# Attention and two mixture-of-experts layers on one core: the last unit's input weighted ahead of its split, its last chunk added and stored in one step, q's scale inside its exponential, and another list of steps

## The chip, the cores and the metric

The kernel runs on one core of one Trainium2 chip. The metric is the device time of one execution in microseconds. The kernel before took 541.41, 538.64 and 541.26 us in three runs; the median is 541.26 us.

## What is computed

Three layers follow each other. The first is a linear attention over 4 batches, 8 heads, 576 tokens and a head size of 64, with 128 random features. The second and third are mixtures of 8 experts over the 2304 tokens, in which each token goes through the one expert that its gate prefers:

```python
q_s, k_s = (q * scale, k * scale)
def phi(x):
    proj = np.einsum('bhsd,md->bhsm', x, omega)
    sq = np.sum(x * x, axis=-1, keepdims=True) / 2.0
    h = proj - sq
    h = h - np.max(h, axis=-1, keepdims=True)
    return np.exp(h) / np.sqrt(m)
kv = np.einsum('bhsm,bhsd->bhmd', k_p, v)
num = np.einsum('bhsm,bhmd->bhsd', q_p, kv)
den = np.einsum('bhsm,bhm->bhs', q_p, z)[..., None] + 1e-06
...
for e in range(E):
    h = np.maximum(x[mask] @ w1[e], 0.0)
    ye = h @ w2[e]
    out[mask] = gate_w[mask, None] * eom[mask, e, None] * ye
```

The last line is that of the second layer; the third has the same without `eom`. An expert's matrices are 512 x 1024 and 1024 x 512.

## The kernel before, in words

**Attention.** Two heads of a batch make a `Pair`; there are 16, named 0 to f in the list of steps. A pair is loaded (a, b, c for q, k, v), projected on `om` (the features, scaled by `head_dim ** -0.25`; k in `k_proj`, L184, q in `q_proj`, L218), q's projections are copied out of PSUM (r), their maximum over the partitions is taken on POOL (t), subtracted on DVE (s, L229) and put through an exponential on ACT (x, L233); k goes through a maximum (m, L194) and an exponential (e, L198). Then come the products with v (v), the quotient (n, d, L285 to L289), the turn into the layout of the experts (f, g, `xraw`), and the split of that into a high and a low part (h, l), since the experts' products are made of three fp32r terms: high x high, low x high, high x low.

**Experts.** The most chosen expert of a batch is run on all 576 tokens of that batch as dense work; a table of ones and weights, `cb`, multiplies its result, so that tokens of other experts get zero. Such a run is a `Unit`. There are 8, one per layer and batch, in the order `(0,0) (0,1) (1,0) (1,1) (0,2) (0,3) (1,2) (1,3)`; unit 7, the last, takes its input from unit 5. A unit takes 64 steps of 6 TensorE matmuls of 128x128 by 128x288 each (`run`, L495 to L534): 32 steps up, in 16 groups of 2, and 32 steps down, in 8 groups of 4. Each group fills one of two PSUM banks (`pm`). After an up group ACT takes `hh` out of the bank (L514) and DVE `hl` (L515); after a down group DVE multiplies the bank with `cb` into `y` (L533). A bank is used again two groups later. The weights come in 8 pieces for a unit: fetched (F), cast to the high part `wh` (H, on ACT, or on DVE where the step has a plus, L130 and L132), and their low part `wl` subtracted on DVE (L, L487).

**The tables and the splits.** A gate (flow G) works out a unit's weights on the tokens; its last pieces are small DVE operations (L410 to L424), a transposition on TensorE (`ptc`, L428), a copy to SBUF on ACT (`ct`, L431) and a store to DRAM (`cohd`, L433). Step W (`weigh`, L489) then loads `cb` from `cohd`, spread over all partitions. Both transfers are issued by SP. A first-layer unit's `y` is split for the second layer by X (high, `next_high`) and Y (low, `next_low`, L543).

**The rest.** Tokens that do not go through their batch's chosen expert are gathered into small blocks (flows A and B); in the last unit their results are added to `y` (L758 for the other batches, `merge`, L547 for unit 7's own batch), and `store` (L556) writes the output.

**What sets the order.** `PLAN` is a list of step names that the program walks once; each name emits its instructions on all engines, a number n lets the units' work go on by n steps, `zN` spends N idle matmuls. Each engine runs its own instructions in the order in which they were emitted, and waits in that order; SP does so with the transfers.

Of the kernel before, what the change touches and what calls it, by code (L numbers as in the profile page):

```python
# [23 lines left out]
NF = 128  # L24
# [17 lines left out]
CW = 2 * HD + 4  # L42
TERMS = (0, 0), (0, 1), (1, 0)
# [16 lines left out]
o6 h5 l5 2 f70 g70 f71 q80 q81 r801 ab g71+ G1 G1 o7 r800 r810 h6+ l6 h7+ l7 r811 1 G1 t80 G1 1 t81 S020 G1 G1 2 s80  # L60
# [34 lines left out]
def attention_moe_moe_kernel(ctx, tc, qT, kT, vp, omst, wg1, wg2, w1a, w2a, w1b, w2b, tabs, eye, outT):  # L95
# [41 lines left out]
    class Pair:  # L137
# [667 lines left out]
    with tc.manual_schedule():  # L805
# [54 lines left out]
        for n, u in enumerate(units):  # L860
# [103 lines left out]
```

## Time and profile before

| | |
|---|---|
| runs | 541.41, 538.64, 541.26 us (median 541.26) |
| the profiled execution | 542.26 us, its span on the core 540.4 us |
| TensorE | busy 98% of the span, 5292 matmuls |
| DVE, ACT, POOL | busy 63%, 36%, 13% |

The profile is one execution. Its span is the time from the core's first instruction to its last; the execution's own time has 1.9 us more around it. Busy shares are means over the whole span; the attention ahead of the first unit (the first 54 us) and the units behind it have different limits, so the stretches are to be read apart.

### The profile page before, as it was taken

To read this page: it belongs to the slowest core of one execution; us is meant where nothing else is said; L and a number is where in the kernel's file an instruction comes from. 1 tells how busy PE (TensorE), PEld (TensorE's weight loads), DVE (VectorE), ACT (ScalarE), POOL (GpSimd) and SP (SyncE) were. 2 spreads that over 40 slices of the span, in tenths; PEclk is the share of its full clock that TensorE was granted. 3 is DMA by queue.
4 is the path that set the end of the run, shared out by engine and by line. 5 is a ranking of instruction groups with operands and counts; after the bars stand their busy time and mean duration, and the time that the engine had idled before them with its cause. 6 is when DMAs were issued, how large, how long until landed. Compare 5 with 4: busy or idle time off the path is not lost.

```text
span 540.4 us, 12927 instructions
## 1 busy us (share of the span) xinstructions
PE 529.9 (98%) x5292; PEld 504.7 (93%) x5292; DVE 342.3 (63%) x772; ACT 192.1 (36%) x490; POOL 72.9 (13%) x68
## 2 busy tenths in 40 slices
PE   9999999999999999999999999999999999999995
PEld 6877999899999999999999999999999999999994
DVE  4999663885667867468643456766674368574532
ACT  5887431335325555133320034432330233023100
POOL 5651102230010323020000000500000000021100
PEclk9999999999999999999999999999999999999998
DMA  8547641264426844037234530116425522859421
GB/s 292 186 136 207 194 142 40 90 176 130 102 70 212 253 152 120 30 124 223 92 92 147 128 96 13 55 69 180 124 54 172 174 63 81 269 156 356 162 83 49
DMA packets 83955, 74.18 MB, mean 137 GB/s; under 512 B 14256, under 2 KB 68144, under 8 KB 83888
## 3 DMA queue, kind: packets, MB, share of 16 engines
q1 hardware_dynamic: 83600, 73.15, 43.5%
q8 instruction: 43, 0.70, 0.5%
q14 instruction: 24, 0.20, 0.1%
q10 hardware_dynamic: 288, 0.13, 0.1%
HBM read 57.79 MB, written 15.48 MB: 136 GB/s over the span
## 4 chain that ended last, share of the span: by engine, by line
PE 85%; DVE 8%; DMA 3%; ACT 1%; issue 1%; POOL 1%; POOLq 0%; DVEq 0%
PE pm L91 71%; PE ph L218 3%; PE pn L267 3%; PE ph L184 3%; PE pkv L241 2%; DVE nm L194 2%; DVE qhh L229 1%; DVE wl L487 1%; PE pg L338 1%; DMA wr<-w1a 1%; PE pf L303 1%; DMA wr<-w1b 1%; DMA om<-omst 1%; DVE xt L289 1%; ACT kp L198 0%
## 5 line engine op out<-in xcount | busy, mean ns | idle before, releaser
L91 PE MATMUL pm<-hh,wh 128*128 128x288 f32 x512 | 153.6, 300 | 0.3 <-DVE y L533 0.3
L91 PE MATMUL pm<-xh,wh 128*128 128x288 f32 x512 | 153.0, 299 | 0.3 <-DVE hl L515 0.2
L91 PE MATMUL pm<-xh,wl 128*128 128x288 f32 x512 | 151.0, 295 | 0.0
L91 PE MATMUL pm<-hh,wl 128*128 128x288 f32 x512 | 150.8, 295 | 0.0
L91 PE MATMUL pm<-hl,wh 128*128 128x288 f32 x512 | 150.8, 295 | 0.0
L91 PE MATMUL pm<-xl,wh 128*128 128x288 f32 x512 | 150.8, 294 | 0.0
L515 DVE SCALAR_TENSOR_TENSOR hl<-pm,hh 128x288 fp32r<-128x288 f32 x128 | 58.5, 457 | 83.6 <-ACT hh L514 83.1
L225 POOL PARTITION_ALL_REDUCE qhl<-qhh x32 | 65.0, 2068 | 284.7 <-DVE qhh L130 100.8
L514 ACT ACTIVATE hh<-pm 128x288 fp32r<-128x288 f32 x128 | 52.6, 412 | 137.1 <-PE pm L91 137.0
L91 PEld LDWEIGHTS pm<-xh,wh 128*128 128x128 f32 x512 | 96.1, 188 | 3.9 <-issue 1.6
L91 PEld LDWEIGHTS pm<-hh,wh 128*128 128x128 f32 x512 | 96.1, 188 | 3.3 <-issue 1.8
L91 PEld LDWEIGHTS pm<-hl,wh 128*128 128x128 f32 x512 | 96.1, 188 | 0.0
L91 PEld LDWEIGHTS pm<-xl,wh 128*128 128x128 f32 x512 | 96.1, 188 | 0.0
L91 PEld LDWEIGHTS pm<-xh,wl 128*128 128x128 f32 x512 | 96.1, 188 | 0.0
L91 PEld LDWEIGHTS pm<-hh,wl 128*128 128x128 f32 x512 | 96.0, 188 | 0.0
L487 DVE TENSOR_TENSOR wl<-wr,wh 128x1024 fp32r<-128x1024 f32 (+1 forms) x72 | 79.8, 1120 | 3.2 <-ACT wh L132 2.7
L533 DVE TENSOR_TENSOR y<-pm,cb 128x288 f32<-128x288 f32 x64 | 29.0, 454 | 69.2 <-PE pm L91 63.8
L132 ACT CAST wh<-wr 128x1024 fp32r<-128x1024 f32 (+1 forms) x39 | 36.9, 960 | 51.4 <-PE pm L91 32.2
L198 ACT ACTIVATE kp<-ph,nm 128x128 f32<-128x128 f32 x140 | 39.3, 385 | 12.9 <-DVE nm L194 12.9
L194 DVE TENSOR_REDUCE nm<-ph 128x3 f32<-128x384 f32 (+1 forms) x64 | 27.7, 483 | 4.1 <-PE ph L184 3.9
L229 DVE TENSOR_TENSOR qhh<-qhh,qhl 128x576 f32<-128x576 f32 x32 | 28.9, 907 | 1.0 <-POOL qhl L225 0.9
L233 ACT ACTIVATE qhh<-qhh 128x576 f32<-128x576 f32 x32 | 22.2, 697 | 15.4 <-DVE qhh L229 15.4
(128 smaller groups left out, 435.8 us busy)
## 6 DMA issues: line engine op xcount, KB each, us to landing
wr<-w2a SPq DMA_DIRECT2D x16, 512.0 KB, 3.8
wr<-w2b SPq DMA_DIRECT2D x16, 512.0 KB, 4.5
wr<-w1a SPq DMA_DIRECT2D x12, 512.0 KB, 4.2
wr<-w1b SPq DMA_DIRECT2D x12, 512.0 KB, 4.7
vt<-vp SPq DMA_DIRECT2D x16, 325.0 KB, 4.3
qr<-qT SPq DMA_DIRECT2D x16, 288.0 KB, 3.6
kr<-kT SPq DMA_DIRECT2D x16, 288.0 KB, 4.6
xd<-xraw SPq DMA_DIRECT2D x16, 288.0 KB, 3.0
```

The costliest lines, as they stand in the source:

```text
L91: nc.tensor.matmul(out, ws(*t), xs(*t), start=first and t == terms[0], stop=last and t == terms[-1])
L132: nc.scalar.copy(out=out, in_=in_)
L184: nc.tensor.matmul(pk[j][:, i * NF : (i + 1) * NF], self.kr[r, c0 : c0 + 128], om[r, :], start=True, stop=True)
L194: nc.vector.tensor_reduce(out=nm[:, j, 0:m], in_=pk, axis=AX.X, op=ALU.max, negate=True)
L198: nc.scalar.activation(self.kp[:, c, j * NF : (j + 1) * NF], self.pk[part][j][:, i * NF : (i + 1) * NF], AF.Exp, bias=self.nm[part][:, j, ...
L225: nc.gpsimd.partition_all_reduce(qm, qe, 128, bass_isa.ReduceOp.max)
L229: nc.vector.tensor_tensor(out=qe, in0=qe, in1=qm, op=ALU.subtract)
L233: nc.scalar.activation(qe, qe, AF.Exp)
L487: nc.vector.tensor_tensor(out=wl[:, p], in0=self.raw[i][:, p], in1=wh[:, p].bitcast(F32), op=ALU.subtract)
L514: nc.scalar.activation(hh[:, s], pm, AF.Relu)
L515: nc.vector.scalar_tensor_tensor(out=hl[:, s], in0=pm, scalar=0.0, in1=hh[:, s].bitcast(F32), op0=ALU.max, op1=ALU.subtract)
L533: nc.vector.tensor_tensor(out=y[:, t], in0=pm, in1=self.cb[:, t], op=ALU.mult)
```

## The change

The multiplication of `om` by the scale goes to a copy, `omk`, which only k's projection uses; q is projected on `om` as it is loaded, and its exponential takes `scale=SCALE`. Unit 5's four chunks of `y` are multiplied by unit 7's `cb` (new steps C50 to C53, in place) ahead of their split, so unit 7 needs no multiplication behind its down groups: of its four chunks the first three are copied out of PSUM by ACT, and the last is added straight from PSUM to the block's result and written to `y` in the one operation of `merge`. `cb` gets a second buffer. All else is the list: nearly every step stands in another place.

```diff
-a0 I a1 b0 b1 c0 c1 c2 J a2 a3 a4 b2 b3 b4 b5 c3 c4 c5 z14 q00 q01 k00 r001 r010+ k01 r000 t00 r011+ m00 t01 q10 r101+
...
+a0 I z14 q00 b0 r001 r000+ q01 b1 k00 k01 r010 t00 r011 a1 m00 e000 q10 r100+ z8 q11 r101+ e001 m01 e010 r110 e011 s00
...
-                        pk[j][:, i * NF : (i + 1) * NF], self.kr[r, c0 : c0 + 128], om[r, :], start=True, stop=True
+                        pk[j][:, i * NF : (i + 1) * NF], self.kr[r, c0 : c0 + 128], omk[r, :], start=True, stop=True
...
-            nc.scalar.activation(qe, qe, AF.Exp)
+            nc.scalar.activation(qe, qe, AF.Exp, scale=SCALE)
...
-            self.cb = pl.mp.tile([128, S], F32, tag="cb", name="cb", bufs=1)
+            self.cb = pl.mp.tile([128, S], F32, tag="cb", name="cb", bufs=2)
...
-                    nc.vector.tensor_tensor(out=y[:, t], in0=pm, in1=self.cb[:, t], op=ALU.mult)
+                    if self is not units[-1]:
+                        nc.vector.tensor_tensor(out=y[:, t], in0=pm, in1=self.cb[:, t], op=ALU.mult)
+                    elif c < NDC - 1:
+                        nc.scalar.copy(out=y[:, t], in_=pm)
+                    else:
+                        self.merge(block, c, t, pm)
                     yield
+
+        def scale(self, c):
+
+            y = self.y[c]
+            nc.vector.tensor_tensor(out=y, in0=y, in1=units[-1].cb, op=ALU.mult)
...
-        def merge(self, block, c, t):
-            y = self.y[c][:, t]
+        def merge(self, block, c, t, y=None):
+            out = self.y[c][:, t]
             nc.vector.scalar_tensor_tensor(
-                out=y, in0=block.y[c][:, t], scalar=state[:, 8], in1=y, op0=ALU.mult, op1=ALU.add
-            )
+                out=out, in0=block.y[c][:, t], scalar=state[:, 8], in1=out if y is None else y, op0=ALU.mult, op1=ALU.add
+            )
...
-            nc.vector.tensor_scalar(out=om, in0=om, scalar1=float(HD) ** -0.25, scalar2=None, op0=ALU.mult)
+            nc.vector.tensor_scalar(out=omk, in0=om, scalar1=SCALE, scalar2=None, op0=ALU.mult)
...
+                    if u.b == units[-1].b:
+                        steps[f"C{n}{c}"] = partial(u.scale, c)
```

By engine the list's instructions come to 502 on ACT in place of 493 and 766 on DVE in place of 773; TensorE has the same matmuls and 23 idle ones in place of 25. The experts' matmuls stand in 51 uninterrupted stretches on TensorE in place of 49.

**First place: DVE around the split of the first unit's first weights** (`wh` and `wl`; the rows on `gt`, `g` and `done` are the end of the first unit's gate, those on `rd` and `xt` the last pair's quotient of batch 0). Before:

```order
L194 TENSOR_REDUCE nm<-ph 128x2 x2
L410 TENSOR_REDUCE gt<-ge 72x8
L411 TENSOR_SCALAR gt<-gt 72x8
...
L424 TENSOR_TENSOR g<-g,gt 72x64
...
L289 TENSOR_TENSOR xt<-pn,rd 128x256
L130 CAST wh<-wr 128x512 x2
L487 TENSOR_TENSOR wl<-wr,wh 128x512 x2
L130 COPY xraw<-pf 128x192
L130 COPY qhh<-ph 128x288 x2
L487 TENSOR_TENSOR wl<-wr,wh 128x1024
L515 SCALAR_TENSOR_TENSOR hl<-pm,hh 128x288 x2
```

and in the change:

```order
L290 TENSOR_TENSOR xt<-pn,rd 128x256
L131 CAST wh<-wr 128x512 x2
L488 TENSOR_TENSOR wl<-wr,wh 128x512 x2
L411 TENSOR_REDUCE gt<-ge 72x8
L412 TENSOR_SCALAR gt<-gt 72x8
...
L425 TENSOR_TENSOR g<-g,gt 72x64
L131 COPY xraw<-pf 128x384
L516 SCALAR_TENSOR_TENSOR hl<-pm,hh 128x288
L488 TENSOR_TENSOR wl<-wr,wh 128x1024
L516 SCALAR_TENSOR_TENSOR hl<-pm,hh 128x288
```

The seven gate operations (two shown, four left out, one shown) now stand behind the split of the first piece, and the low part of the second piece stands behind the first group's `hl`. Two casts of `xh<-xraw` that DVE did ahead of this place are on ACT in the change.

**Second place: ACT in the first unit**, where `ct` is copied. Before:

```order
L431 COPY ct<-ptc 64x72
L132 COPY xraw<-pf 128x384
L132 COPY xraw<-pf 128x192
L132 COPY xraw<-pf 128x384
L132 CAST wh<-wr 128x1024
L132 COPY qhh<-ph 128x288
L514 ACTIVATE hh<-pm 128x288 x2
```

and in the change:

```order
L133 CAST wh<-wr 128x1024
L133 COPY qhh<-ph 128x288
L515 ACTIVATE hh<-pm 128x288 x10
L133 CAST wh<-wr 128x1024
L515 ACTIVATE hh<-pm 128x288 x5
L133 CAST wh<-wr 128x1024
L432 COPY ct<-ptc 64x72
L133 CAST wh<-wr 128x1024
L515 ACTIVATE hh<-pm 128x288
```

The copy of `ct` stood ahead of the unit's first group; now it stands behind the fifteenth of its 16 up groups and a weight cast.

**Third place: DVE in the last down groups of unit 6**, between two multiplications of a bank. In the change:

```order
L131 CAST xh<-y 128x576
L554 TENSOR_TENSOR xl<-y,xh 128x576
L535 TENSOR_TENSOR y<-pm,cb 128x288
L488 TENSOR_TENSOR wl<-wr,wh 128x1024 x2
L643 SCALAR_TENSOR_TENSOR order<-ones 128x576
L648 TENSOR_SCALAR sel<-bx,state 128x576
L651 SCALAR_TENSOR_TENSOR order<-ones,sel 128x576
L535 TENSOR_TENSOR y<-pm,cb 128x288
```

Before, these operations had more multiplications between them:

```order
L533 TENSOR_TENSOR y<-pm,cb 128x288
L633 SCALAR_TENSOR_TENSOR order<-ones 128x576
L487 TENSOR_TENSOR wl<-wr,wh 128x512 x2
L543 TENSOR_TENSOR xl<-y,xh 128x576
L533 TENSOR_TENSOR y<-pm,cb 128x288 x2
L487 TENSOR_TENSOR wl<-wr,wh 128x1024
L533 TENSOR_TENSOR y<-pm,cb 128x288 x2
L638 TENSOR_SCALAR sel<-bx,state 128x576
L641 SCALAR_TENSOR_TENSOR order<-ones,sel 128x576
```

Two weight splits and the three operations of a block's ranking (`order`, `sel`) now stand between one multiplication and the next.

## Rows read from the trace of the kernel before

**Rows 1.** Page, part 1: busy us (share of the span) and count by engine.

```profile
PE 529.9 (98%) x5292; PEld 504.7 (93%) x5292; DVE 342.3 (63%) x772; ACT 192.1 (36%) x490; POOL 72.9 (13%) x68
```

**Rows 2.** Stretches: us, busy PE, PEld, DVE, ACT, POOL; PEclk, DMA share, GB/s.

```profile
20.00:40.00 20.00, 19.35 (x375) 16.07 (x375) 18.79 (x49) 17.68 (x57) 11.45 (x6) 1.00 0.37 123
40.00:54.30 14.30, 13.47 (x264) 11.04 (x260) 13.64 (x46) 10.79 (x39) 2.22 (x2) 1.00 0.67 200
```

**Rows 3.** Chain of waits, start and first unit: start us, us, what.

```profile
4.20 0.24 DVE om L822
...
48.60 5.97 DMA wr<-w1a
54.60 1.06 ACT wh L132
55.68 1.87 DVE wl L487
57.55 0.38 DVE hl L515
57.97 33.65 PE pm L91 x252
91.62 1.20 PE ph L218 x8
```

**Rows 4.** TensorE behind two waits: idle time and its end in brackets.

```profile
57.97 0.40 PE L91 MATMUL pm<-xh,wh 128*128 128x288 f32 x1 [0.22 <-DVE hl L515]
...
514.50 0.40 PE L91 MATMUL pm<-hh,wh 128*128 128x288 f32 x1 [0.34 <-DVE y L533]
```

**Rows 5.** Chain of waits at the end of the span.

```profile
533.88 0.47 DVE y L533
534.35 0.02 issue
534.38 0.52 DVE y L547
```

**Rows 6.** Groups on DVE: busy us, mean ns; idle before, what ended it.

```profile
L487 DVE TENSOR_TENSOR wl<-wr,wh 128x1024 fp32r<-128x1024 f32 x56 | 69.7, 1245 | 3.1 <-ACT wh L132 2.7
L533 DVE TENSOR_TENSOR y<-pm,cb 128x288 f32<-128x288 f32 x64 | 29.0, 454 | 69.2 <-PE pm L91 63.8 <-DMA xd<-y 3.9 <-PE pc L380 1.3
L543 DVE TENSOR_TENSOR xl<-y,xh 128x576 fp32r<-128x576 f32 x16 | 11.7, 750 | 3.1 <-ACT xh L132 3.0
L130 DVE CAST xh<-xraw 128x576 fp32r<-128x576 f32 x8 | 3.6, 452 | 0.6 <-ACT xraw L132 0.5
L641 DVE TENSOR_TENSOR_SCAN order<-ones,sel 128x576 f32<-128x576 f32 x1 | 1.4, 1359 | 0.0
```

**Rows 7.** DVE in order of time, 49 to 51 us: start us, us, operation.

```profile
49.23 0.20 DVE L410 TENSOR_REDUCE gt<-ge 72x8 f32<-72x64 f32 x1
...
50.44 0.22 DVE L424 TENSOR_TENSOR g<-g,gt 72x64 f32<-72x64 f32 x1
```

**Rows 8.** Groups on ACT.

```profile
L514 ACT ACTIVATE hh<-pm 128x288 fp32r<-128x288 f32 x128 | 52.6, 412 | 137.1 <-PE pm L91 137.0
L132 ACT CAST wh<-wr 128x1024 fp32r<-128x1024 f32 x31 | 32.5, 1047 | 40.9 <-PE pm L91 21.7 <-DMA wr<-w1b 14.6 <-DMA wr<-w1a 4.4
L431 ACT COPY ct<-ptc 64x72 f32<-64x72 f32 x8 | 1.7, 210 | 6.5 <-PE ptc L428 6.5
```

**Rows 9.** Stores of the gates' tables, source L433.

```profile
L433 SPq DMA_DIRECT2D cohd<-ct x8: 484/494/596, 51.3 to 447.6; - x8
...
DMA to landing us min/median/max: 1.7/3.9/5.5
```

**Rows 10.** Loads and readers of `cb`.

```profile
L533 DVE TENSOR_TENSOR y<-pm,cb x64: 437/457/458, 83.7 to 533.9; 128x288 f32<-128x288 f32 x64
...
DMA to landing us min/median/max: 3.9/4.5/7.1
```

**Rows 11.** Output stores, source L556.

```profile
DMA to landing us min/median/max: 1.9/2.6/7.2
```

More of the change, by code (lines that the diff above doesn't have):

```diff
@@ L42 @@
 CW = 2 * HD + 4
+SCALE = float(HD) ** -0.25
 TERMS = (0, 0), (0, 1), (1, 0)
@@ new lines @@
+S320 re01 re11 te1 xd1 ke1 xd0 L46 re00 re10 te0 2 S330 me1 ee11 2 ee10 nd0 nd1 dd0 se1 H47 se0 ce qf0 qf1 rf01 rf00
+rf10 kf0 kf1 dd1 tf0 rf11 mf0 xe0 tf1 mf1 ef11 ef10 1 L47 ef01 o9 ob 3 ef00 sf0 1 ve0 ve1 xf0 cf vf0 vf1 xe1 sf1 S110
+we+ ne0 xf1 wf+ ne1 nf0 nf1 fd0 de0 fd1 de1 df0 df1 2 gd0 gd1 hd ld fe0 ff0 ff1 gf0 gf1+ fe1 ge0 ge1+ he+ 1 G5 G5 1 of
+G5 G5 1 G5 G5 1 le hf lf 4 P5 G5 1 G5 2 F50 F51 H50+ L50 F52 4 S430 H51 L51 oc 4 H52 L52 G5 3 S400 2 G5 1 F53 H53+ 2
+S420 4 F54 L53 2 F55 G5 3 od 5 H54+ H55+ 2 X40 L54 L55 1 W5 1 F56 Y40 2 G6 H56+ L56 3 F57 X41+ G6 G6 G6 2 Y41 2 G6
@@ L86 @@
+M710 B S710 B B B B B B M700 M720 S720 S700 1 4
 """
@@ L543, in next_low, with fetch_back @@
             nc.vector.tensor_tensor(out=xl, in0=self.y[c], in1=xh.bitcast(F32), op=ALU.subtract)
-        def merge(self, block, c, t):
-            y = self.y[c][:, t]
+        def merge(self, block, c, t, y=None):
+            out = self.y[c][:, t]
             nc.vector.scalar_tensor_tensor(
-                out=y, in0=block.y[c][:, t], scalar=state[:, 8], in1=y, op0=ALU.mult, op1=ALU.add
+                out=out, in0=block.y[c][:, t], scalar=state[:, 8], in1=out if y is None else y, op0=ALU.mult, op1=ALU.add
             )
+        def fetch_back(self, c, t):
+            src = outT[c * 128 : (c + 1) * 128, self.b * S + t.start : self.b * S + t.stop]
+            nc.sync.dma_start(out=self.y[c][:, t], in_=src)
         def store(self, c, t=slice(0, S)):
@@ L556, in store @@
             nc.sync.dma_start(out=dst, in_=self.y[c][:, t])
-        def fetch_back(self, c, t):
-            src = outT[c * 128 : (c + 1) * 128, self.b * S + t.start : self.b * S + t.stop]
-            nc.sync.dma_start(out=self.y[c][:, t], in_=src)
     def left(l):
@@ L809, in attention_moe_moe_kernel @@
         om = const.tile([128, NF], F32, name="om")
+        omk = const.tile([128, NF], F32, name="omk")
         zeros = const.tile([128, 256], BF16, name="zeros")
@@ L870, in attention_moe_moe_kernel @@
                     steps[f"S{n}{c}{s}"] = partial(u.store, c, t)
-                    if last:
+                    if last and c < NDC - 1:
                         steps[f"M{n}{c}{s}"] = partial(u.merge, block, c, t)
                 if u.l == 0:
+                    if u.b == units[-1].b:
+                        steps[f"C{n}{c}"] = partial(u.scale, c)
                     steps[f"X{n}{c}"], steps[f"Y{n}{c}"] = partial(u.next_high, c), partial(u.next_low, c)
```

68 lines of the change are left out of this document (31 added, 37 removed).

## The prediction, made before the change was timed

> **What bounds the kernel now.** I read the engines' busy shares first. TensorE is busy 98% of the span and DVE 63%, ACT 36% [rows 1]. The reader is to see there that only work taken off TensorE, or time in which it stands still, can move the end by much; the change takes no matmul off it but two idle ones. So the question is where TensorE waits, and I went on to the stretches and the chain of waits.
>
> Ahead of the first unit the picture is another one. From 20 to 54 us DVE is busy 18.79 of 20.00 and 13.64 of 14.30 us, ACT 17.68 of 20.00 [rows 2]. TensorE's busy share is high there too, but its matmuls are small and many of them hang on DVE's and ACT's results. The chain enters the experts by a landing of weights at 54.6 us, a cast on ACT (1.06 us), the subtraction on DVE (1.87 us, more than one piece of work) and `hl`; only then, at 57.97 us, comes TensorE's long stretch: 252 matmuls in 33.65 us, 0.1335 us each [rows 3]. A step of six is then 0.80 us, a down group of four steps 3.20 us. From there on the chain is TensorE's, with small gaps. Two of them stand out: 0.22 us behind `hl` at 57.97 and 0.34 us behind `y` at 514.50 [rows 4]. Behind the last matmul come a multiplication (0.47 us), a handover (0.02) and the addition (0.52), and then the last store [rows 5].
>
> The profiled execution took 542.26 us, 1.0 above the median of 541.26. The sum is made against 542.26 and then shifted by 1.0. A measurement of this kernel tells about 0.5%, or 2.7 us, from no change.
>
> **The change part by part.**
>
> *The attention's end.* Three things leave DVE ahead of the first weights' split. The scaling of `om` leaves the path to the first q projection: 0.24 us [rows 3]. Two casts of `xh` go to ACT: 2 x 0.452 = 0.9 us [rows 6]. The gate's last seven operations go behind the split: from 49.23 to 50.66 us, 1.4 us [rows 7]. That is 2.5 us of DVE. The first two pay in full if DVE is the limit, 1.1 us. The third pays only as far as the first piece of weights has landed, since DVE would else stand before it; no row says how early it lies there, but its fetch follows the gate's choice, which comes 0.9 us earlier for the same two casts. I take -2.0, nearer to the whole, as both stretches have DVE at 94 and 95%. The ends are -2.5 and +1.2: ACT gets two casts that, by the 1.047 us of a cast of 1024 columns [rows 8], are some 0.6 us each, and it is busy 88% of the first stretch.
>
> *The wait at 57.97.* The second piece's subtraction moves behind the first group's `hl`, so this wait of 0.22 us goes, with the slow restart behind it: the matmul took 0.40 us by its row. I take -0.4 (ends -0.5 and 0, where the next `hl` is late instead: it now stands behind the subtraction, with one more bank to cover it).
>
> *The last unit's first multiplication.* The wait of 0.34 us at 514.50 goes, because ACT copies the bank (0.41 us by the `hh` row, the same shape [rows 8]) where DVE stood behind a run of additions: -0.5 with the restart. The eight multiplications themselves lay beside TensorE and cost nothing before; the six copies are covered in the same way, by the other bank's 3.20 us. Were the cover gone, one copy would cost its 0.41 us.
>
> *Unit 0's table, the new wait.* Before, the first store of `ct` began at 51.3 us, and `y` first read `cb` at 83.7 [rows 9, 10]. Now the copy of `ct` stands on ACT behind the fifteenth `hh` and a weight cast, so it starts only when 30 of the unit's steps are done. From there: `hh` 0.41, cast 1.05, copy 0.21 [rows 8], store 3.9 [rows 9], load 4.5 [rows 10], multiplication 0.45 [rows 6], and some 0.3 for six handovers at 0.02 to 0.05 us, 10.8 us in all. TensorE can go on until it needs the first down group's bank back, at the end of step 40: 60 matmuls at 0.1335 are 8.0 us, the last pair's q projection that now stands between them is 1.2 (the row at 91.62 [rows 3]), with the changes of work 9.3 us. The stall is 10.8 - 9.3 = +1.5. Behind the waiting multiplication DVE has copies of q's projections and of `kvr`, and TensorE's next work hangs on them, so nothing fills the gap; on SP the loads of the next weights stand behind the table's load, but those are due more than 20 steps later. With the shortest transfers (1.7 and 3.9 us) the chain is 8.0 us and the stall 0; with the longest (5.5 and 7.1) it is 15.0 and the stall +5.7. I take the medians.
>
> What the Trainium skill says of this differs. Its page "DMA: Bandwidth & Descriptors", section "Anatomy of one DMA — SWDGE (gpsimd) path", fits a transfer's time by 2.0 us plus its bytes over 436 GB/s; as an estimate from that page the 18 KB store would take 2.0 and the 295 KB load 2.7 us, there would be no stall, and the sum would be 1.5 us lower. The rows of this case show 3.9 and 4.5, and I go by these.
>
> *More stretches.* TensorE goes two more times from attention to experts' matmuls and back. By the waits above a change costs some 0.1 us each way in idle and restart: +0.4 (0 to +0.9, two waits of 0.22 with their restarts).
>
> *DVE late in unit 6.* Between one multiplication and the next now stand two subtractions and the ranking's three operations: 2 x 1.245 + 2 x 1.36 and, for `sel`, the 0.45 of a cast of the same tile [rows 6], 5.7 us. TensorE has two groups of 3.20 = 6.4 us from the end of one group until it needs that bank's successor back; DVE needs 0.45 + 5.7 + 0.45 = 6.6. The excess of 0.2 and a restart of 0.2 to 0.3 make +0.5 (0, if DVE starts part of it early, to +1.4, if it also waits for the cast of 1.05 behind which the subtractions come).
>
> *The weighting ahead.* Unit 7's table must now be there before unit 5's `y` is split. In the list its transposition ends at step 407 of 512; copy 0.2, an `hh` before it 0.4, store and load 8.4, the multiplication at 0.75 (the row of `xl`, the same tile), a cast 0.6, the subtraction 0.75 [rows 6], unit 6's own `y` behind them 0.45, handovers 0.3: 11.9 us. TensorE needs that `y` by the end of step 424, 17 steps or 13.6 us later. So nothing, with +2.5 as the upper end (12.6 for the two transfers). The second buffer of `cb` is what lets it be loaded while unit 6's is in use.
>
> *The end.* One multiplication of 0.47 and its handover of 0.02 go from the chain behind the last matmul [rows 5]: -0.5. The ends are 0 and -1.2, if the last store also lands at the 1.9 us of the quickest instead of 2.6 [rows 11]. The additions for the other batches and the three whole-chunk merges, seven operations at 0.75, 5.3 us, stand ahead of the last chunk's merges; the block's last product is in the list 15 steps, 12.0 us, before the end, and the first of these merges is due 3.2 us before it, which leaves 3.5 us for POOL between.
>
> *The sum.* -2.0 - 0.4 - 0.5 + 1.5 + 0.4 + 0.5 - 0.5 = -1.0. From 542.26 that is 541.3, and against the median 540.3. This is no change that can be measured.
>
> **The rivals.**
>
> *Faster: the front gives all, and the table is in time.* The front's whole 2.5 in place of 2.0 and a stall of 0 in place of 1.5 give 540.3 - 0.5 - 1.5 = 538.3, just past the bound of 538.55. For it: in eight transfers of each kind the shortest pair leaves 1.3 us of room, and the part of the sum that is only a restart may be nothing. Against it: the medians are above. The Trainium skill's fit for a transfer, named above, is on its side.
>
> *Slower: the table is late by its slowest.* Store and load stand on SP beside fetches of 512 KB weights. With 5.5 and 7.1 us the stall is 5.7 and the time 540.3 + 4.2 = 544.5, with all behind the multiplication on DVE late as well. For it: both of these durations were seen. Against it: in two columns of eight they are the worst. It decides from where the two transfers take 12.1 us together (a stall of 5.2); from 6.9 us on there is a stall at all.
>
> *ACT takes DVE's place in the front.* It is busy 88% there and gets 1.2 us more; then the front is +1.2 in place of -2.0 and the time 543.5, still within the bound. Against it: the chain enters by way of DVE, and ACT is busy only 10.79 of the 14.30 us ahead of the first weights [rows 2].
>
> **How the numbers follow.** The forecast gets 0.40, the rival that is faster 0.30, the late table 0.20, ACT in the front 0.10. Faster by over 0.5% is then 0.30, slower by over 0.5% 0.20, and no change 0.40 + 0.10 = 0.50. The range goes down to 537.0, which is the faster rival with 0.7 more at the last store and 0.6 less for the lump on DVE and the stretches, and up to the late table's 544.5; what lies beyond, a table late in both units or a front that loses and gains at once, I hold for 2 in 10 or less.
>
> **What would show it.** In the changed kernel's profile the first experts' matmul should start about 52.3 us, some 2 before the 54.3 that end the second stretch of now, with no wait of TensorE for `hl` two groups later. A wait of TensorE for `y` of 1 to 2 us should stand near the 40th step of unit 0, ended by a load of `cb`. Late in unit 6 TensorE should wait for `y` for under 1 us. Behind the last matmul one DVE operation of 0.5 us should stand where two stood. If the attention is as long as before, or no wait for `cb` shows in unit 0, the terms -2.0 or +1.5 are wrong; a wait for `y` at another place, which none of these terms has, would make the whole wrong.

## The result: 0.8% slower, and the profile after

The changed kernel took 544.66 us (median of ten runs, 543.66 to 545.47); the kernel before, run beside it ten times, 539.44 (538.64 to 542.20). The ratio is 1.0083, 95% interval 1.0064 to 1.0102: slower by 4.5 us, where 540.3 and no change were forecast. The time lies 0.2 us above the range.

The ten runs of the kernel before also show that the execution profiled before, 542.26 us, was slower than all of them, 2.8 us above their median. A second profile of it (`before_again`, below) fell on one of 539.47 us. The ledger is made against that one; "experts" is from the first to the end of the last expert matmul, "behind" from there to the end of the span.

| us | before, profiled first | before, second profile | changed | changed less second |
|---|---|---|---|---|
| first experts' matmul | 54.31 | 54.19 | 54.36 | +0.2 |
| experts | 479.55 | 479.06 | 481.25 | +2.2 |
| behind | 6.54 | 4.45 | 6.89 | +2.4 |
| span | 540.4 | 537.7 | 542.5 | +4.8 |

So the loss has two halves, in the experts' stretch and behind the last matmul, and the attention gave nothing. The +0.2 of the first row is scatter: the six profiles that start with the old list have that matmul at 53.99 to 55.46 us, the six that start with the new one at 53.80 to 54.78. Of the +2.4 behind the last matmul 1.1 is the later issue of the last store, 1.8 is that it landed 3.5 us behind its issue where the second profile has 1.7, and -0.5 is the rest. The same landing took 3.8 us in the first profile of before, so it is not shown that the change made it slower. The page of the changed kernel shows none of it (parts 1 and 4):

```profile
PE 531.0 (98%) x5290; PEld 505.4 (93%) x5290; DVE 341.2 (63%) x765; ACT 194.1 (36%) x499; POOL 74.6 (14%) x68
PE 88%; DVE 7%; DMA 2%; ACT 1%; issue 1%; SPq 0%; POOL 0%; DVEq 0%; ACTq 0%; POOLq 0%
```

The shares are those of [rows 1]. What differs is where TensorE stands between two experts' matmuls. TensorE in order of time, changed kernel, the matmul behind each of four new waits (a fifth, at 206.56, reads as a start of 206.97 where 206.69 was due; the trace names no wait there):

```profile
246.40 0.40 PE L92 MATMUL pm<-xh,wh 128*128 128x288 f32 x1 [0.45 <-DVE y L535]
278.21 0.40 PE L92 MATMUL pm<-hh,wh 128*128 128x288 f32 x1 [0.42 <-DVE hl L516]
430.35 0.40 PE L92 MATMUL pm<-xh,wh 128*128 128x288 f32 x1 [0.18 <-DVE hl L516]
481.13 0.40 PE L92 MATMUL pm<-xh,wh 128*128 128x288 f32 x1 [0.47 <-DVE y L535]
```

From one matmul's start to the next's these places take 0.74, 0.72, 0.47 and 0.76 us, and the fifth 0.42, in place of 0.13. The waits of [rows 4] are gone. What stood ahead of them differs from place to place. DVE ahead of the first:

```profile
241.55 1.63 DVE L131 CAST wh<-wr 128x1024 fp32r<-128x1024 f32 x1
243.22 1.23 DVE L488 TENSOR_TENSOR wl<-wr,wh 128x1024 fp32r<-128x1024 f32 x1
244.36 0.75 DVE L230 TENSOR_TENSOR qhh<-qhh,qhl 128x576 f32<-128x576 f32 x1
245.03 0.75 DVE L554 TENSOR_TENSOR xl<-y,xh 128x576 fp32r<-128x576 f32 x1
245.88 0.82 DVE L535 TENSOR_TENSOR y<-pm,cb 128x288 f32<-128x288 f32 x2
```

The bank's multiplication stands behind 4.3 us of other work, and both `y` come at once. Of the 4.3 us 0.95 are in no list of steps: the cast takes 1.63 us where the others of its shape take 0.68 to 0.69, though the last weights fetched ahead of it had landed at 235.86. It lies within a maximum that POOL takes over the partitions:

```profile
241.07 2.85 POOL L226 PARTITION_ALL_REDUCE qhl<-qhh  x1
```

A smaller cast at 239.06 (1.37 us where the others take 0.42) lies within the maximum ahead of it (238.75 to 241.17), and each of the two casts ends 0.74 us before its maximum does. In `after_mended` the larger cast comes at 244.41, behind POOL's work, and takes 0.68. That POOL's work holds the cast is as far as these rows go; no run tests it alone. Without the 0.95 us the multiplication would have been in time, since TensorE waited for 0.45.

At 277.1 a gate's copy on ACT, which waits for DVE, stands ahead of the bank's `hh` (the same at 205.4), and at 429.2 a cast on DVE that waits for its weights stands ahead of `hl`:

```profile
277.10 0.26 ACT L367 COPY ls<-pt 72x128 f32<-72x128 f32 x1 [2.04 <-DVE top L366]
429.24 0.69 DVE L131 CAST wh<-wr 128x1024 fp32r<-128x1024 f32 x1 [1.02 <-DMA wr<-w1b]
```

The DVE rows of the last place stand under "Why the prediction was wrong".

Behind the last matmul, the end of the chain of waits, first of the kernel before (second profile), then of the changed kernel:

```profile
513.90 19.34 PE pm L91 x144
...
533.27 0.47 DVE y L533
...
533.76 0.52 DVE y L547
```

```profile
523.67 11.94 PE pm L92 x90
...
535.63 0.52 DVE y L558
```

One operation stands where [rows 5] had two, as forecast. But the last stores, on SP, kernel before (second profile) and changed kernel (the first number is the first issue, the second reaches to the end of the last):

```profile
532.47 2.17 SPq L556 DMA_DIRECT2D outT<-y  x2
534.30 0.33 SPq L556 DMA_DIRECT2D outT<-y  x1
```

```profile
532.27 0.81 SPq L572 DMA_DIRECT2D outT<-y  x2
...
537.31 0.92 SPq L572 DMA_DIRECT2D outT<-y  x2
```

Before, the last store is issued at 534.30, in the moment its addition ends (533.76 + 0.52). Now the addition ends at 536.15, and the two final stores go out at 537.31 and 537.77: SP comes too late. These two stand in the program behind a branch (the fallback that is not taken), and SP's last store ahead of it was issued at 532.65. The trace has SP's comparison for the branch at 533.13 to 533.18 and its next instruction at 536.49; in the second profile of before they are at 528.64 to 528.70 and 531.65.

### The profile page after: what moved, and what is told of

Its sections match the earlier page's. It is cut to its first block, busy times and chain, and to the rows that moved or that the text cites. A ratio compares the mean times of both kernels' runs of the same rounds, so it can differ in the third digit from the quotient of the medians.

```text
span 542.5 us, 12911 instructions
## 1 busy us (share of the span) xinstructions
PE 531.0 (98%) x5290; PEld 505.4 (93%) x5290; DVE 341.2 (63%) x765; ACT 194.1 (36%) x499; POOL 74.6 (14%) x68
## 4 chain that ended last, share of the span: by engine, by line
PE 88%; DVE 7%; DMA 2%; ACT 1%; issue 1%; SPq 0%; POOL 0%; DVEq 0%; ACTq 0%; POOLq 0%
PE pm L92 70%; PE pn L268 3%; PE ph L185 3%; PE pkv L242 3%; PE ph L219 3%; PE pf L304 2%; DVE wl L488 2%; PE pg L339 1%; DVE nm L195 1%; DMA wr<-w1b 1%; DVE qhh L230 1%; DVE wh L131 1%; DMA kr<-kT 1%; PE idle L852 1%; PE pu L707 0%
## 5 line engine op out<-in xcount | busy, mean ns | idle before, releaser
L226 POOL PARTITION_ALL_REDUCE qhl<-qhh x32 | 67.1, 2138 | 280.2 <-ACT qhh L133 137.0
L488 DVE TENSOR_TENSOR wl<-wr,wh 128x1024 fp32r<-128x1024 f32 (+1 forms) x72 | 81.1, 1142 | 7.5 <-ACT wh L133 7.2
L133 ACT CAST wh<-wr 128x1024 fp32r<-128x1024 f32 (+1 forms) x33 | 32.0, 972 | 58.5 <-DMA wr<-w1b 20.8
L535 DVE TENSOR_TENSOR y<-pm,cb 128x288 f32<-128x288 f32 x56 | 25.3, 454 | 42.1 <-PE pm L92 39.4
L199 ACT ACTIVATE kp<-ph,nm 128x128 f32<-128x128 f32 x140 | 41.2, 396 | 7.6 <-DVE nm L195 7.3
L131 DVE CAST wh<-wr 128x1024 fp32r<-128x1024 f32 (+1 forms) x39 | 25.5, 666 | 7.0 <-DMA wr<-w2b 2.8
```

Of the source, the lines that this page charges most:

```text
L131: nc.vector.tensor_copy(out=out, in_=in_)
L133: nc.scalar.copy(out=out, in_=in_)
L199: nc.scalar.activation(self.kp[:, c, j * NF : (j + 1) * NF], self.pk[part][j][:, i * NF : (i + 1) * NF], AF.Exp, bias=self.nm[part][:, j, ...
L226: nc.gpsimd.partition_all_reduce(qm, qe, 128, bass_isa.ReduceOp.max)
L488: nc.vector.tensor_tensor(out=wl[:, p], in0=self.raw[i][:, p], in1=wh[:, p].bitcast(F32), op=ALU.subtract)
L535: nc.vector.tensor_tensor(out=y[:, t], in0=pm, in1=self.cb[:, t], op=ALU.mult)
```

## The experiments

Ratios are to the kernel before in runs on the same chip, with 95% intervals; a profile's numbers are those of one execution. Of each list of steps some of the tokens that differ are shown.

**before_again.** No edit.

> The kernel before, unchanged, for a second profile. Ten runs of it lie at 538.6 to 542.2 us, median 539.4, and the first profile was taken of one at 542.3, so the sum rested on an execution 2.8 us above the median. Theory 1 (the time between quick and slow executions lies ahead of the experts, where the weights' landing at 54.6 us ended the wait): a quick execution starts its experts some 2 us sooner, at about 52, and the rest is the same. Theory 2 (it lies behind the last matmul, in the last store's landing): first experts' matmul at 54.3 as before, and the time behind the last matmul 5 us in place of 6.8. Ratio to itself 1.000 within 0.003.

Measured: 539.7 us, ratio 1.0002 (0.9987 to 1.0016), profile of 539.47. The experts start at 54.19 in place of 54.31 us; the last store lands 1.7 us after its issue in place of 3.8; the wait at 57.97 of [rows 3, 4] is not there, the second piece of weights having landed at 54.13 in place of 54.58. So most of the 2.7 us between the two spans lies behind the last matmul (theory 2), 0.5 in that wait. The wait that the prediction counted as -0.4 comes in some executions and not in others: of the six profiles that start with the old list, late_store's and code_spread_a's have it too.

**list_only.** The new list with the old arithmetic.

```diff
-            nc.vector.tensor_scalar(out=omk, in0=om, scalar1=SCALE, scalar2=None, op0=ALU.mult)
+            nc.vector.tensor_scalar(out=om, in0=om, scalar1=SCALE, scalar2=None, op0=ALU.mult)
...
-                    if self is not units[-1]:
...
+                    nc.vector.tensor_tensor(out=y[:, t], in0=pm, in1=self.cb[:, t], op=ALU.mult)
-A 1 C50 A X50
+A 1 A X50
...
-S720 S700 1 4
+S720 S700 1 M730 4 M731
```

> The new list of steps with the old arithmetic: om scaled in place, no weighting ahead, the last unit multiplied by cb behind its down groups, its last chunk multiplied and then added. Theory 1 (the list costs the time: DVE's order in the experts' groups and the ending): 544 to 546 us, as slow as the changed kernel or 0.5 slower. Theory 2 (the changed arithmetic costs it, by the weighting on DVE ahead of the split): 540 to 541 us.

Measured: 548.98 us, 1.0170 (1.0148 to 1.0191). Slower still than either theory had it: the list is what costs, and without the new arithmetic it is worse by 4 to 5 us more. In its profile 1.6 of them lie in the experts' stretch and 2.0 behind the last matmul's start (9.2 us in place of 7.2), where the multiplications that are back on DVE hold up the block's additions.

**code_only.** The new arithmetic with the old list.

```diff
-G7 L66 F70
+G7 W7 L66 F70
...
-H67+ X50 Y50 1 X51 1 Y51 X52+ 2 A 1 L67 F71 2 Y52 X53+
+H67+ C50 X50 Y50 1 C51 X51 1 Y51 C52 X52+ 2 A 1 L67 F71 2 Y52 C53 X53+
...
-S630 W7 H73
+S630 H73
```

> The new arithmetic with the old list (only the table's load W7 moved ahead behind its gate, C50 to C53 put straight ahead of X50 to X53, and M730 and M731 gone). Theory 1 (the list costs the time): 538.5 to 540 us, at the kernel before or up to 0.9 quicker, for the wait at 514 us (0.5) and one operation behind the last matmul (0.5) go. Theory 2 (the arithmetic costs it): 543 to 545 us, with TensorE waiting for y of unit 6 where the weighting stands on DVE.

Measured: 543.14 us, 1.0062 (1.0045 to 1.0079). Theory 2's number, but not its reason: three weightings stand in a row ahead of one multiplication of unit 6, two of them with a split that waits for ACT, and TensorE waits 2.46 us (TensorE in order of time):

```profile
460.04 0.40 PE L92 MATMUL pm<-hh,wh 128*128 128x288 f32 x1 [2.46 <-DVE y L535]
```

Behind that wait its clock falls (stretches; the eighth number is the granted clock):

```profile
450.00:457.00 7.00, 7.00 (x55) 7.00 (x54) 5.35 (x20) 1.09 (x3) 0.00 (x0) 1.00 0.45 108
460.00:463.90 3.90, 3.86 (x17) 3.86 (x18) 3.83 (x9) 0.00 (x0) 0.00 (x0) 0.56 0.31 91
```

Of the next 16 intervals between matmuls 15 are 0.24 us. The run was confounded by where I had put the steps; code_spread repeats it.

**after_old_end.** The changed kernel, its last 64 steps by the old list.

```diff
-S630 10 F73 F74 1 H73+ 2 L73 F75
+F73 F74 S600 S620 S630 H73 2 L73 F75
...
-B B B B B M710 B S710 B B B B B B M700 M720 S720 S700 1 4
+B 1 B 1 L77 7 M700 S700 8 M710 8 M720 7 S710 S720
```

> The changed kernel up to step 448 of 512 and from there the old list's ending (last unit; the stores of unit 6's first and third chunk and two weight fetches set at its start). Theory 1 (the new ending costs: SP issues its last planned store 2.5 us ahead of the last addition and reaches the final stores only 4 us later, at 537.3, 1.2 us behind the addition that they wait for, and DVE's ranking stands ahead of y): the final stores are issued as soon as their addition is done, and the time is 1.5 to 2.5 us shorter than the changed kernel's, 542 to 543. Theory 2 (the loss lies in the units before and ahead of them): 544.5, as the changed kernel.

Measured: 542.11 us, 1.0052 (1.0033 to 1.0072), 1.7 us less by the ratios, whose intervals just overlap; behind the last matmul's start 4.0 us in place of 7.2. The last store goes out as soon as its addition is done, and lands in 1.9 us in place of 3.5. Theory 1, with 0.6 us given back at the joint (an interval of 0.77 us at 433.8).

**code_spread.** code_only with the weightings spread.

```diff
-C50 X50 Y50 1 C51 X51 1 Y51 C52 X52+ 2 A 1 L67 F71 2 Y52 C53 X53+ 1 H70
+C50 X50 Y50 4 A C51 1 L67 F71 X51 2 Y51 1 H70
...
-A A 1 L70 F72 1 Y53 5 S610 H71 2 L71 F73 6 S620
+A A C52 1 L70 F72 3 X52+ Y52 3 S610 H71 1 C53 1 L71 F73 3 X53+ Y53 3 S620
```

> The new arithmetic with the old list, as in code_only, but the four weightings and splits of unit 5's chunks spread over the steps 416 to 437, behind unit 6's multiplications, where code_only had three of them in a row ahead of one (TensorE stood 2.75 us at 457.3 us there, and its next 16 matmuls came at 0.24 us in place of 0.13, some 1.7 us more). Theory 1 (the arithmetic is worth its two terms, 0.5 us for the wait at 514 us and 0.5 for the operation behind the last matmul): no such wait, and 538.5 to 539.0 us, 0.6 to 1.1 below the kernel before. Theory 2 (the weighting ahead costs as much on DVE as it saves): 539.6 or more, with a new wait for y in unit 6.

Measured: 538.1 us, 0.9966 (0.9950 to 0.9981): faster than the kernel before by 1.8 us (1.0 to 2.7), more than its two terms. No wait in unit 6 beyond 0.35 us. DVE at the end, one operation for each half of the last chunk:

```profile
529.01 0.52 DVE L558 SCALAR_TENSOR_TENSOR y<-by,state,pm 128x288 f32<-128x288 f32 x1 [1.91 <-PE pm L92]
532.21 0.52 DVE L558 SCALAR_TENSOR_TENSOR y<-by,state,pm 128x288 f32<-128x288 f32 x1 [2.68 <-PE pm L92]
```

Against the second profile of before the experts start 0.2 us sooner, their stretch is 0.9 shorter and what lies behind 0.4. The arithmetic is a gain; the list is what lost it.

**after_mended.** The changed kernel, five places of its list mended.

```diff
-ed11 G3 1 ed10 2 md0
+ed11 2 G3 ed10 1 md0
...
-L30 H31+ L31 tc0
+L30 tc0
...
-gb0 6
+gb0 H31+ L31 6
...
-oa G4 1 H35+ 2 L35
+oa 1 H35+ G4 2 L35
...
-oe H62+ F63 1 L62 F64 2 H63+ 2 S510
+oe F63 1 H62+ 2 L62 F64 2 S510 H63+
...
-A A L72 A A 2 S610 3 A 2 S630 10 F73
+A A A A 2 S610 5 S630 A 2 L72 8 F73
```

> The changed kernel with its list mended at the five places where TensorE waited 0.42 to 0.76 us between two matmuls of the experts (206.6, 245.7, 277.5, 429.9 and 480.4 us): at each the one operation on DVE or ACT that stood ahead of the bank's own is put behind it; the ending is left. Theory 1 (these waits cost what they measure: five intervals of 3.1 us in all less 5 x 0.13, and 0.1 at each restart): 2.5 to 2.9 us below the changed kernel, about 542. Theory 2 (they are slack given back before the end, since the ending waits for the stores): 544, as the changed kernel.

Measured: 542.97 us, 1.0058 (1.0037 to 1.0080), 1.7 us below the changed kernel by the medians, 1.35 by the ratios, in place of 2.5 to 2.9. All five waits are gone from its trace, and the last matmul starts at 533.37 in place of 535.30, 1.9 sooner, though two waits for `hl` in unit 0 (intervals of 0.30 and 0.45 us at 57.5 and 62.6) took 0.5 back in that execution. From the last matmul's start to the end nothing changed (7.1 us in place of 7.2). Theory 1, with part given back; the intervals of the two ratios overlap, so it rests on the trace more than on the time.

**front_moves.** The kernel before with the attention's two moves alone.

```diff
-h0+
+h0
...
-h2+
+h2
...
-e711 G0 w6 e701 d50 d51 f40 f41 G0 G0 G0 g40
+e711 w6 e701 d50 d51 f40 f41 g40
...
-L00 F02 g50 g51+ o5 W0
+L00 F02 G0 g50 g51+ o5 G0 G0 G0 W0
```

> The kernel before with the two moves of the attention's end that the prediction counted at -2.0 us, and nothing else: two casts of xh from DVE to ACT, and the first gate's last seven DVE operations with its table behind the split of the first weights. Theory 1 (TensorE's own work is the limit there: in the quick execution the chain's last 3.2 us ahead of the experts are TensorE's): first experts' matmul at 54.0 to 54.4 us as before (54.2), time within 0.5 us of the kernel before. Theory 2 (DVE is the limit, as the prediction had it): first experts' matmul at 52 to 52.7 us, and 1.5 to 2 us less.

Measured: 544.06 us, 1.0076 (1.0051 to 1.0102), the experts starting at 57.20. Neither theory: two new waits. The chain of waits ahead of the experts:

```profile
53.09 1.28 DVE wl L487 x2
54.38 0.14 DVE gt L410
...
55.88 0.22 PE ptc L428
56.10 1.17 PE ph L218 x8
```

The gate's transposition, which I had left ahead of the last pair's projection, held TensorE's queue until the moved operations were done. The other wait is the cast on ACT. The next two runs take the moves apart.

**front_xh.** Two casts of `xh` on ACT.

```diff
-h0+
+h0
...
-h2+
+h2
```

> The kernel before with one of the two moves of the attention's end alone: the casts of xh of the first and third pair on ACT in place of DVE. In front_moves, where both moves were made, the chain had the second of these casts (0.56 us) between two exponentials of k on ACT, and TensorE's pn that follows started at 38.68 in place of 37.54 us. Theory 1 (ACT, not DVE, has no room at that place): first experts' matmul at 54.9 to 55.4 us in place of 54.2, and 0.7 to 1.2 us more time. Theory 2 (DVE is the limit of the front, as the prediction had it): 53.3 and 0.9 less.

Measured: 541.79 us, 1.0030 (1.0014 to 1.0045), the experts at 55.22: 1.0 later. The chain of waits, front_xh and then the kernel before (second profile):

```profile
34.24 1.91 ACT kp L198 x7
36.15 0.56 ACT xh L132
36.71 0.78 ACT kp L198 x3
...
38.55 0.93 PE pn L267 x24
```

```profile
33.78 2.18 ACT kp L198 x9
...
36.05 0.43 ACT kp L198
...
37.54 0.93 PE pn L267 x24
```

The cast stands in the middle of the exponentials that TensorE waits for. The other cast is on this chain as well, at 19.52 us (0.67 us on ACT), and the chain is 0.46 us late ahead of the rows shown. The start of the experts alone would prove little, since the same list start scatters by 1.5 us; the ratio is clear of 1. ACT has no room there: theory 1.

**front_gate.** The gate's tail behind the split, its transposition at step 10.

```diff
-e711 G0 w6 e701 d50 d51 f40 f41 G0 G0 G0 g40
+e711 w6 e701 d50 d51 f40 f41 g40
...
-L00 F02 g50 g51+ o5 W0
+L00 F02 G0 g50 g51+ o5
...
-L02 F04 6 H03
+L02 F04 3 G0 2 G0 G0 W0 1 H03
```

> The kernel before with the other move alone: the first gate's last seven DVE operations behind the split of the first weights, its transposition on TensorE at step 10 and the copy, store and load of the table at step 12 (in front_moves the transposition stayed ahead of the first experts' matmul and held TensorE until 55.9 us). Theory 1 (TensorE is the limit of the last 3 us ahead of the experts): first experts' matmul at 54.0 to 54.3, the time within 0.5 us of the kernel before. Theory 2 (DVE is the limit, by the 1.4 us that the seven operations take): 52.8 and 1.4 less. No wait for the table in either, since it is read only from step 36 on.

Measured: 540.01 us, 1.0001 (0.9987 to 1.0015). The profiled execution started its experts at 53.54, 0.65 sooner, and ended 0.45 sooner (539.02 against 539.47 us); the twelve runs show none of it. By the interval the gain is at most 0.7 us: not theory 2.

**late_store.** The kernel before with one addition and store moved to the end.

```diff
-8 M710 8 M720 4 M730 3 S710 S720 M731
+8 M710 12 M730 3 S710 M731 M720 S720
```

> The kernel before with one addition and store of the last unit (third chunk) put behind the last addition. The five traces so far have 4.2 to 4.7 us from SP's last planned store to the first of the two final stores, behind the program's branch. Theory 1 (SP needs these 4.2 us whatever the additions do, so the list's ending must have SP's last planned store 4 us ahead of the last addition): that store is issued at about 535, the two final stores at 539.3 and 539.7, and the time is 5 us longer, about 544.6. Theory 2 (the final stores were only waiting for their additions): 540, one store longer.

Measured: 545.47 us, 1.0095 (1.0068 to 1.0122). SP, the moved store and then the final two:

```profile
536.53 0.33 SPq L556 DMA_DIRECT2D outT<-y  x1
...
540.75 0.81 SPq L556 DMA_DIRECT2D outT<-y  x2
```

Their additions had long been done. From SP's last store ahead of the branch to the first behind it: 4.22 us here, 4.22 in before's second profile, 4.21 in code_only, 4.23 in after_old_end, 4.66 in the changed kernel, and 5.12 in list_only, where issuing the last store ahead of the branch alone took 1.23. Counted from the end of that issue it is 3.9 us in fourteen of the sixteen profiles and 4.2 in those of the changed kernel and after_mended. Theory 1: SP needs this time whatever else is done, and before it lay beside TensorE's last matmuls.

**mended_old_end.** after_mended's first four mended places with the old list from step 440.

```diff
-H71 L71 1 A H72 A A L72 A A 2 S610 3 A 2 S630 10 F73 F74 1 H73+ 2 L73 F75
+H71 L71 S610 F73 S600 S620 1 A A A A A 2 H72+ A 1 L72 F74 3 A 1 S630 H73 2 L73 F75
...
-B B B B B M710 B S710 B B B B B B M700 M720 S720 S700 1 4
+B 1 B 1 L77 7 M700 S700 8 M710 8 M720 7 S710 S720
```

> The changed kernel with four of the five mended places (those ahead of step 440) and the old list's ending from there, which has SP's last planned store 4 us ahead of the last addition. Theory 1 (the changed kernel's loss is these waits, some 2 us, and the ending, some 2.5 us, and nothing else): 539 to 540 us, level with the kernel before. Theory 2 (something else in the new list costs as well): 541 or more.

Measured: 542.19 us, 1.0047 (1.0030 to 1.0064). Inconclusive: the joint put a cast, a subtraction and the ranking ahead of one multiplication, with intervals of 1.75 and 0.95 us at 477.8 and 481.0.

**mended_old_end2.** The same, spread.

```diff
-H72+ A 1 L72 F74 3 A 1 S630 H73 2 L73
+H72+ 2 A 1 A 2 S630 H73 1 L72 F74 1 L73
```

> mended_old_end with the ranking's operations and one subtraction spread around the steps 445 to 449, so that no multiplication of unit 6 has more than 4 us of other work on DVE ahead of it. Theory 1 (the waits and the ending are all of the changed kernel's loss): no wait of more than 0.4 us in the experts, 4 us behind the last matmul, 539 to 540.2 us, level with the kernel before. Theory 2 (something else in the new list costs as well): 541 or more.

Measured: 541.19 us beside 540.70, ratio 1.0011 (0.9999 to 1.0023). The median is 1.0 above the range that was expected, but the kernel before stood 1.3 higher in these runs too; by the ratio it is level or up to 1.2 us above, and its profile has new waits that were not expected, of 1.34 us for `y` at 483.93, at the joint, and of 1.92 for `hl` at 438.98. The run puts back the old list from step 440 on, and not the ending alone. So the waits ahead of that step and the list behind it are the loss, to within about a microsecond.

**code_spread_a.** code_spread, one step moved.

```diff
-F70 1 A 3 A
+F70 2 A 2 A
```

> code_spread with one step of the block's choice (three small operations on DVE, 0.2 us each) put behind the hl of step 412 instead of ahead of it, for the wait of 0.35 us that is left at 449 us. Theory 1 (DVE's order there sets the wait): the interval is 0.13 to 0.24 us and the time 0.2 to 0.3 below code_spread's 538.1, too little to tell by time alone. Theory 2 (the weights' subtraction ahead of it is enough): the wait stays.

Measured: 538.23 us, 0.9962 (0.9946 to 0.9978). The interval of 0.35 us at 449 us is gone, so DVE's order set it; the time is that of code_spread.

**code_spread_gate.** code_spread with front_gate's move.

```diff
-L00 F02 g50 g51+ o5 W0
+L00 F02 G0 g50 g51+ o5
...
-L02 F04 6 H03
+L02 F04 3 G0 2 G0 G0 W0 1 H03
```

> code_spread with the first gate's tail behind the split of the first weights, as in front_gate, where the experts started at 53.5 us in place of 54.2 but the time did not tell (1.0001, 0.9987 to 1.0015). Theory 1 (that start was the scatter of single executions, which lies between 54.0 and 55.5 for the same front): 538.1 as code_spread. Theory 2 (the move is worth 0.6 us): 537.5, ratio 0.995.

Measured: 538.08 us, 0.9958 (0.9941 to 0.9975). The profiled execution started its experts at 53.62 and then waited 0.97 us more at 56.8. The time is code_spread's: theory 1. The three code_spread versions beat the kernel before, by 1.8 to 2.3 us.

## Why the prediction was wrong

**The base.** The sum shifted its result by 1.0, to a median of three. The profiled execution was 2.8 us above the median of ten. The wait at 57.97 and the slow landing of the last store set it apart from the second profile. With the median of ten the same sum would have read 538.4, further off still.

**"I take -2.0, nearer to the whole, as both stretches have DVE at 94 and 95%."** This step failed; it measured +0.2, which is nothing beside the scatter. The two stretches after, to be read with [rows 2]:

```profile
20.00:40.00 20.00, 19.48 (x377) 16.55 (x374) 18.65 (x45) 18.80 (x60) 10.60 (x6) 1.00 0.15 50
40.00:54.30 14.30, 13.34 (x255) 10.48 (x252) 13.01 (x40) 10.52 (x37) 3.37 (x2) 1.00 0.77 246
```

ACT has 1.1 us more in the first, as forecast; DVE has 0.1 and 0.6 less, of the 2.5 forecast; and the end stayed. In [rows 2] TensorE is as busy as DVE (97 and 94% beside 94 and 95%), so the shares do not say which of them the end waits for. The chain of waits of the changed kernel does, for the last 5.7 us ahead of the experts:

```profile
48.77 1.39 PE pn L268 x40
50.16 2.33 PE pkv L242 x80
52.49 0.69 PE ph L219 x4
53.18 1.25 PE pf L304 x7
54.43 0.59 PE pm L92 x3
```

They are TensorE's own. So the gate's tail was worth nothing there (front_gate: at most 0.7 us), and the casts, moved in the old list, put the experts 1.0 us later by way of ACT (front_xh). Further back DVE is on the chain of the changed kernel too (3.8 us from 40.07 on), and the scaling of `om` was not tried alone; what the rest of the new order gave or took there stays open. The rival "ACT takes DVE's place" had the mechanism, with +1.2 where front_xh shows +1.6 (0.8 to 2.4) for that edit alone; the new list as a whole did not pay it.

**The wait at 57.97, -0.4.** It is not in the changed kernel's profile, but nor is it in the second profile of before, so the ledger has nothing for it. Of the five other profiles that start with the new list, three have intervals of 0.30 to 0.45 us for `hl` at 57.5 to 62.7.

**The table of unit 0, +1.5.** It measured nothing. The chain was the one described: SP's two transfers, and DVE's multiplication waiting for the load:

```profile
80.27 0.56 SPq L434 DMA_DIRECT2D cohd<-ct  x1
82.10 0.39 SPq L492 DMA_DIRECT2D cb<-cohd  x1
```

```profile
86.36 0.46 DVE L535 TENSOR_TENSOR y<-pm,cb 128x288 f32<-128x288 f32 x1 [1.98 <-DMA cb<-cohd]
```

DVE stood 1.98 us, but the store took 1.8 us, not the 3.9 of [rows 9], and the load 4.2, not 4.5. With these two the prediction's chain is 8.4 us, against the 9.3 that it gives TensorE, so no stall is left. The step at fault is "I take the medians". Over the changed kernel's eight units the two read:

```profile
DMA to landing us min/median/max: 1.7/2.3/3.6
...
DMA to landing us min/median/max: 3.9/4.2/5.9
```

The estimates from the Trainium skill's fit ("DMA: Bandwidth & Descriptors", "Anatomy of one DMA — SWDGE (gpsimd) path") were 2.0 and 2.7 us, by a fit for transfers that GpSimd issues, where SP issues these: the store agrees with it here, the load does not. The rival "slower: the table is late" was the wrong mechanism for the right sign.

**The last unit's first multiplication, -0.5**, was right, and so was the arithmetic as a whole: code_spread has it with the operation saved at the end.

**The lump late in unit 6, +0.5.** The size was right, the place one multiplication early. Behind the five operations that the sum lists TensorE lost nothing new (an interval of 0.27 at 478.57, where the second profile of before has 0.25). The interval of 0.76 at 480.4, 0.63 more than without a wait, hangs on the next multiplication, ahead of which stand three more operations of the block's ranking, 2.0 us, that the sum does not have. DVE there, changed kernel:

```profile
476.99 1.36 DVE L651 TENSOR_TENSOR_SCAN order<-ones,sel 128x576 f32<-128x576 f32 x1
478.26 0.43 DVE L535 TENSOR_TENSOR y<-pm,cb 128x288 f32<-128x288 f32 x1
478.61 0.45 DVE L656 TENSOR_SCALAR order<-order 128x576 f32<-128x576 f32 x1
479.10 0.76 DVE L659 TENSOR_TENSOR sel<-sel,order 128x576 f32<-128x576 f32 x1
479.89 0.82 DVE L660 SCALAR_TENSOR_TENSOR sel<-order,state,sel 128x576 f32<-128x576 f32 x1
480.62 0.45 DVE L535 TENSOR_TENSOR y<-pm,cb 128x288 f32<-128x288 f32 x1
```

But such a sum was made for one place alone. Four more places have a wait (206.6, 245.7, 277.5, 429.9: intervals of 2.35 us, 1.8 more than without waits), and the prediction has no term for them; the one for `y` at 246.40 is the sign by which, as it said itself, the whole would be wrong. The list shows the work ahead of each bank's operation: at 206.6 and 277.5, in up groups of 1.6 us, a weight subtraction and the gate's copy on ACT that waits behind it; at 429.9 a cast; at 245.7 some 3.3 us on DVE. It does not show the two things on which the waits at 429.9 and 245.7 hang: the 1.02 us that the first cast waited for its weights and the 0.95 us by which the second was longer.

**"More stretches", +0.4.** From start to start, two experts' matmuls that follow each other take 408.95 us in all, against 406.48 in the second profile, and the rest of the experts' stretch 71.99 against 72.28. So the turns to other work gave 0.3 us back, and the waits are the whole of the +2.2, with the -0.5 of the gone wait in them.

**"One multiplication ... and its handover ... go from the chain: -0.5."** The operation went; the end came 2.4 us later. The step failed in what it looked at: it laid DVE's additions into the time before the last chunk, and they fitted (the last of them ended at 532.25, the first half's came at 532.43). It did not ask when SP, which issues their stores, gets behind the branch, and put nothing for it. The old list had SP there at 532.47 in the second profile, ahead of the last addition; the new one, with block and stores later, at 537.31.

**The sum with what was measured**, against the second profile: +0.2 in front, +2.2 in the experts, +2.4 behind, 4.8, where -1.0 was forecast; the ratio's 4.5 us agrees. The 1.8 us of the landing are in the 4.8; the last store took 3.5 us in after_mended too, with the same ending, and 1.7 to 1.9 in thirteen of the sixteen profiles, so whether the ending made it slow stays open. The runs that undo the parts give: ending undone -1.7, waits mended -1.4, both -3.9 (mended_old_end2), by the ratios.

## What to carry to other kernels

Where a change replaces a whole order of work, lay each engine's queue between two uses of the same buffer against the time that the buffer gives, at every such place and not at the one that looks worst (two of the five waits here hung, beside that, on a landing and on a longer cast that only the trace shows); do it for the DMA-issuing queue at the end of the program too, where a branch ahead of the last stores needs its own lead. Take a limit from the chain of waits that leads into the stretch, not from a busy share that several engines have at once. And profile the kernel before more than once when its runs differ by more than the effect: here one execution's landing and one wait were half as large as the change.

## What the runs showed of the hardware that had not been expected

Between SP's comparison for the untaken block and SP's next instruction behind it 2.9 to 3.0 us pass in fourteen of the sixteen profiles and 3.3 in two (the changed kernel's and after_mended's), and some 0.8 more until the first store, whose addition had always been done by then. That it is the loading of the code behind the branch was not tested.

Two casts on DVE that lay within a maximum over the partitions on POOL took 1.37 and 1.63 us in place of 0.42 and 0.68, and each ended 0.74 us before its maximum did (changed kernel; list_only and after_old_end have the same two to within 0.01 us). Not every cast within such a maximum is longer: one of `xh` in before's second profile, at 20.14 us, took 0.45 as elsewhere. The cause was not tested.

A wait of TensorE of 2.46 us (code_only) was followed by 3.9 us with a granted clock of 0.56, most of it at the lower of its two levels, 1.2 GHz, with matmuls at 0.24 us in place of 0.13, some 1.6 us beyond the wait itself. In mended_old_end2 a wait of 1.92 us was followed, 1.3 us on, by 3.7 us at 0.54; that execution took 543.5 us, where the median of the twelve is 541.2. Behind the waits of 0.2 to 0.5 us of the changed kernel the clock stayed at 1.00, and the matmul intervals beyond the first were 0.13 us.
